# ACT copies a small sum out of the PSUM bank that the transposes share (convolution and two expert layers, one core)

## The chip, the cores and the metric

The kernel runs on one core of one Trainium2 chip. The metric is the device time of one execution in microseconds (us); the median of 3 runs stands for a kernel. The core has TensorE (PE, with its weight loads as PEld), VectorE (DVE), ScalarE (ACT), GpSimd (POOL) and the DMA queues, most of them issued by SyncE (SP). PE writes its results to PSUM, which has eight banks; this kernel gives each of them a fixed use.

## The reference, cut to what matters

```
attn: w = softmax(weight, over 7 taps), one filter per head (8 heads of 24 columns)
      x = causal 7-tap convolution of x[4, 3584, 192] with w          -> 14336 rows x 192
moe:  logits = x @ w_gate;  e = argmax;  gate = softmax(logits)[e]    (8 experts)
      out[row] = gate * (relu(x[row] @ w1[e]) @ w2[e])                w1 192x1024, w2 1024x192
moe2: the same with other weights, and a factor sigmoid(x @ w_output_gate)[e]
```

All arrays are float32. The weights w1 and w2 of both layers (16 experts' worth in all) have to be turned into pairs of 16-bit parts before the products can use them.

## The kernel before, in words

The kernel writes out by hand the order of the instructions on every engine. Each engine executes its own instructions in that order.

**Convolution, passes k = 0 to 36.** A pass multiplies four tiles of 112 rows with a band matrix on PE (`attend(k+1)`, L465). DVE finds each row's largest value and scales the rows (`split(k)`, L479 to L487, which empties the PSUM banks of `attend(k)`). ACT casts the scaled rows to 16 bits (`parts(k-1)`, L493), and POOL forms the low parts (L494, L495). Two passes later PE transposes the rows (`turn(k-3)`, L507), ACT empties the transposes' bank (`evacuate(k-3)`, L510), and PE makes logits (L517). The scaled rows `cxs` have two buffers; the cast rows `chl` have four.

**Slots.** After that the rows, sorted by expert, are worked off in 63 slots of up to 256 rows for each layer, so 126 slots. In slot u PE does `stage1(u)` (40 matmuls into four banks `ph`, L1134); ACT takes the positive part of each bank (L1136) and DVE the remainder (L1137). Then come the background work, `turn2(u-3)` (six transposes of the first layer's results into a bank `tp`, L1186), and `stage2(u-1)` (48 matmuls, L1150), in this order on PE. ACT empties `tp` (`evacuate2`, L1192) after the background work.

**Background work.** Two lists run beside the passes and slots. One routes rows to experts, mostly on DVE. The other prepares the weights of both layers, one unit (w1 or w2 of an expert) at a time: load; largest absolute values by ACT (L298); `scale`, which is `total` and `pow2`; scaling and splitting by ACT, POOL and DVE; store. The 16 units of layer 1 run during the convolution, where `scale` comes between `attend(k+1)` and `turn(k-3)` on PE, ahead of `split(k)` on DVE and ahead of `parts(k-1)` on ACT. The 16 units of layer 2 run during the first layer's slots, one in three slots, where `scale` comes after `stage1(u)` and the routing of that slot, and ahead of `turn2(u-3)`.

**The shared bank.** `total` sums the units' maxima over the 128 partitions with matmuls against ones (L145) into a tile of pool `rps` with tag `lg`. This pool has one buffer per tag. Under the tag `lg` stand `total`, the convolution's logits `lg`, the transposes `tp` of the slots, and the slots' logits `lg2`. Whoever writes next waits until the last reader has read. The first reader of `total` is the first line of `pow2` on DVE (L131, tile `wst`; for the gate weights L133, tile `gbt`).

```
self.rps = self.pool("rps", bufs=1, space=PSUM)
...
u.s, e = self.pow2(wp, self.total([u.am[:, c : c + 1] for c in range(NC)]), [P, 1], "ws")
...
bg(u, "A")
...
turn2(u - 3)
```

Of the kernel before, what the change touches and what calls it, by code (L numbers as in the profile page):

```python
# [11 lines left out]
F32 = mybir.dt.float32  # L12
# [5 lines left out]
P = 128  # L18
# [37 lines left out]
class Kern:  # L56
# [83 lines left out]
    def total(self, ams):  # L140

        n = ams[0].shape[-1]
        r = self.rps.tile([P, n], F32, tag="lg", name="total")
        for i, am in enumerate(ams):
            self.nc.tensor.matmul(r, lhsT=self.ones32, rhs=am, start=i == 0, stop=i == len(ams) - 1)  # L145
        return r

    def setup(self):
        nc = self.nc
# [1298 lines left out]
```

## Time and profile before

| what | value |
|---|---|
| median of 3 runs | 1360.57 us (1359.68 to 1361.41) |
| the profiled execution | 1359.16 us, span of its instructions 1357.2 us |
| PE busy | 1219.5 us, 90% of the span |
| DVE, ACT, POOL busy | 820.9 us, 637.8 us, 616.3 us |
| mean granted TensorE clock | 0.911 |
| convolution passes | from the first `attend` at 16.01 us to the last `evacuate` at 229.59 us |
| first `stage1` | 238.08 us |

The times in a trace count from the first instruction. A row of the timeline gives start and duration, engine, line, operation, the tile written and those read; in square brackets stands how long the engine had been idle before it, and what ended that. A tile's name is the program's with its buffer number left out.

### The profile page before, as it was taken

How to read it: one execution, taken by the hardware profiler on the slowest of the kernel's cores; microseconds unless marked ns; L12 is line 12 of the kernel's file. 1: busy time of each engine (PE TensorE's matmuls, PEld its weight loads, DVE VectorE, ACT ScalarE, POOL GpSimd, SP SyncE). 2: the span in 40 equal slices, each digit the busy share in tenths (PEclk: the TensorE clock that was granted, in tenths of full speed). 3: DMA queues.
4: the chain of work that ended last, by engine and by line, in shares of the span. 5: the costliest groups of instructions: out<-in, count | busy, mean ns of one | idle time of the engine just before them, and what ended most of it. 6: DMA issues, size and time to landing. Idle time of an engine off the chain costs nothing.

```text
span 1357.2 us, 36322 instructions
## 1 busy us (share of the span) xinstructions
PE 1219.5 (90%) x13032; PEld 1153.8 (85%) x13032; DVE 820.9 (60%) x2498; ACT 637.8 (47%) x1155; POOL 616.3 (45%) x673
## 2 busy tenths in 40 slices
PE   5788886979879998988997999999999998999997
PEld 4777776869879888878997999999999997899987
DVE  4777697877664745555457875588664444444442
ACT  2866663345446554665564444433333333333332
POOL 5534444325435544464454534444444446344442
PEclk9755556989889999989998999999999999999999
DMA  6997955555463779558684689765245465756375
GB/s 195 283 282 217 246 150 171 111 134 140 131 170 107 186 203 258 133 151 204 163 206 109 168 177 238 190 115 130 65 120 127 98 134 124 155 138 173 74 189 159
DMA packets 251087, 221.40 MB, mean 163 GB/s; under 512 B 144494, under 2 KB 220839, under 8 KB 250904
## 3 DMA queue, kind: packets, MB, share of 16 engines
q1 hardware_dynamic: 230556, 182.61, 51.3%
q0 software_dynamic: 17136, 34.68, 12.1%
q8 instruction: 106, 1.74, 0.6%
q10 hardware_dynamic: 3212, 1.74, 0.5%
q14 instruction: 77, 0.63, 0.2%
HBM read 275.60 MB, written 60.37 MB: 248 GB/s over the span
## 4 chain that ended last, share of the span: by engine, by line
PE 68%; DVE 19%; issue 4%; DMA 3%; ACT 2%; SPq 2%; POOL 1%; POOLq 0%; DVEq 0%; ACTq 0%
PE ph L1134 30%; PE py L1150 30%; PE cxp L465 4%; DVE h L1137 4%; DVE cxs L487 2%; PE tp L1186 1%; DVE cxp L479 1%; DMA wb<-wd 1%; DMA wb<-wdb 1%; DVE wh L334 1%; PE acc L968 1%; DVE eam L1160 1%; PE total L145 1%; ACT h L1136 1%; DMA mxt<-row 1%
## 5 line engine op out<-in xcount | busy, mean ns | idle before, releaser
L1134 PE MATMUL ph<-mxt,wb 128*128 128x256 f16 (+1 forms) x4840 | 535.2, 270 | 14.8 <-DMA wb<-wdb 6.5
L1134 PEld LDWEIGHTS <-wb 128*128 128x128 f16 x4840 | 455.9, 98 | 67.9 <-issue 9.0
L1150 PE MATMUL py<-wb,h 128*128 128x192 f16 x5592 | 492.5, 249 | 1.6 <-DMA wb<-wd 1.6
L1137 DVE SCALAR_TENSOR_TENSOR h<-ph,h 128x512 f16<-128x512 f32 x476 | 313.4, 686 | 277.2 <-ACT h L1136 273.5
L1150 PEld LDWEIGHTS <-h 128*128 128x128 f16 x5592 | 472.0, 99 | 5.2 <-issue 1.9
L1136 ACT ACTIVATE h<-ph 128x512 f16<-128x512 f32 x476 | 274.3, 595 | 148.4 <-PE ph L1134 143.5
L1050 POOL DMA_INDIRECT row<-rec,idx x238 | 232.1, 975 | 73.3 <-issue 41.0
L1233 POOL DMA_INDIRECT out_dram<-o,io x119 | 120.3, 1011 | 231.0 <-ACT o L1232 199.6
L1169 POOL TENSOR_TENSOR ehl<-exs,ehl 128x256 f16<-128x256 f32 (+1 forms) x63 | 42.6, 677 | 298.5 <-ACT ehl L1168 226.9
L1164 ACT ACTIVATE exs<-py,ess 128x192 f32<-128x192 f32 x119 | 43.9, 417 | 206.6 <-DVE ese L137 202.7
L1232 ACT ACTIVATE o<-py,sc 128x192 f32<-128x192 f32 x119 | 43.9, 417 | 205.6 <-PE py L1150 149.8
L465 PE MATMUL cxp<-x,tz 118*112 118x96 f32 x512 | 94.9, 371 | 38.5 <-DVE cxs L487 29.8
L465 PEld LDWEIGHTS cxp<-x,tz 118*112 118x112 f32 x512 | 88.2, 277 | 41.3 <-DVE cxs L487 31.8
L1160 DVE TENSOR_REDUCE eam<-py 128x2 f32<-128x384 f32 (+1 forms) x63 | 33.6, 533 | 134.9 <-PE py L1150 132.0
L338 POOL TENSOR_TENSOR wh<-wr,wh 128x768 f16<-128x768 f32 x48 | 79.8, 1663 | 50.2 <-ACT wh L326 26.0
L1186 PE MATMUL tp<-ident,ehl 128*128 128x128 f16 x357 | 31.7, 226 | 47.2 <-DVE wst L131 46.5
L510 ACT COPY cxt<-ctp 128x1344 f16<-128x1344 f16 x32 | 40.9, 1277 | 65.8 <-PE ctp L507 65.7
L1192 ACT COPY ext<-tp 128x768 f16<-128x768 f16 (+1 forms) x63 | 47.4, 752 | 46.6 <-PE tp L1186 46.6
L1186 PEld LDWEIGHTS <-ehl 128*128 128x128 f16 x357 | 27.1, 104 | 49.6 <-issue 47.0
L494 POOL TENSOR_TENSOR chl<-cxs,chl 112x512 f16<-112x512 f32 x32 | 40.4, 1261 | 54.1 <-ACT chl L493 43.2
L298 ACT ACTIVATE none<-wr 128x768 f16<-128x768 f32 x64 | 53.8, 840 | 1.0
L517 PEld LDWEIGHTS <-cxt 128*112 128x112 f16 x384 | 35.7, 192 | 5.0 <-issue 4.5
(203 smaller groups left out, 1077.9 us busy)
## 6 DMA issues: line engine op xcount, KB each, us to landing
wb<-wd SPq DMA_DIRECT2D x126, 768.0 KB
wb<-wda SPq DMA_DIRECT2D x126, 512.0 KB
wb<-wdb SPq DMA_DIRECT2D x126, 256.0 KB
wb<-wdb SPq DMA_DIRECT2D x126, 128.0 KB
wr<-in_moe_w_dram SPq DMA_DIRECT2D x16, 768.0 KB
wd<-wh SPq DMA_DIRECT2D x16, 768.0 KB
rec<-chl SPq DMA_DIRECT2D x32, 336.0 KB
rec<-ehl SPq DMA_DIRECT2D x56, 192.0 KB
```

The costliest lines, as they stand in the source:

```text
L298: nc.scalar.activation(none, u.r[:, c * CH : (c + 1) * CH], AF.Abs, scale=scale, accum_out=u.am[:, c : c + 1])
L338: nc.gpsimd.tensor_tensor(u.h[:, 1, q], u.r[:, q], u.h[:, 0, q], ALU.subtract)
L465: nc.tensor.matmul(to[:, :, hh * GD : (hh + 1) * GD], lhsT=self.tz[: self.KI, h, :], rhs=xin[b0][: self.KI, o : o + G, h * GD : (h + 1) * GD],
L1050: nc.gpsimd.indirect_dma_start(out=rw[:, :], out_offset=None, in_=rec[:, :], in_offset=bass.IndirectOffsetOnAxis(ap=idx, axis=0))
L1134: nc.tensor.matmul(ph[:, k, :], lhsT=l, rhs=xt[:, xb, 0:n], start=i == 0, stop=i == 4)
L1136: nc.scalar.activation(hi, ph, AF.Relu)
L1137: nc.vector.scalar_tensor_tensor(lo, in0=ph, scalar=0.0, in1=hi, op0=ALU.max, op1=ALU.subtract)
L1150: nc.tensor.matmul(py[:, c, 0:D], lhsT=h[:, f, a, c * P : (c + 1) * P], rhs=w[:, b, f, :], start=n == 0, stop=n == 3 * NCH - 1)
L1160: nc.vector.tensor_reduce(am, py, axis=AX.X, op=ALU.max, apply_absolute_value=True)
L1186: nc.tensor.transpose(tp[:, 3 * c + b], hl[:, c, b * P : (b + 1) * P], self.ident)
L1192: nc.scalar.copy(xt, self.sl[u].pop("tp"))
L1233: nc.gpsimd.indirect_dma_start(out=outs[q % NOUT][:, :], out_offset=bass.IndirectOffsetOnAxis(ap=io[:, 0:1], axis=0), in_=o, in_offset=Non ...
```

## The change

`total` gets a last step. ACT copies the sums from the PSUM tile to a small tile in SBUF (pool `ew`, four buffers), and `pow2` reads that tile. So the bank's reader is now ACT, and DVE reads the copy. `total` is called 34 times: once for each of the 32 units and once for each of the two sets of gate weights.

```diff
@@ def total(self, ams):
         r = self.rps.tile([P, n], F32, tag="lg", name="total")
         for i, am in enumerate(ams):
             self.nc.tensor.matmul(r, lhsT=self.ones32, rhs=am, start=i == 0, stop=i == len(ams) - 1)
-        return r
+
+        t = self.ew.tile([P, n], F32, tag=f"total{n}", name="sums")
+        self.nc.scalar.copy(t, r)
+        return t
```

## Rows read from the trace of the kernel before

**Rows 1.** Waits of PE, whole span: us in total, times, longest

```profile
PE tp L1186 <- DVE wst L131: 46.5, 16, 9.3
PE cxp L465 <- DVE cxs L487: 29.8, 21, 2.9
```

**Rows 2.** Timeline, the slot with the longest wait: start, us, engine, instruction

```profile
278.63 2.05 ACT L1136 ACTIVATE h<-ph 128x512 f16<-128x512 f32 x4
...
286.81 0.80 PE L1186 MATMUL tp<-ident,ehl 128*128 128x128 f16 x6 [9.33 <-DVE wst L131]
```

**Rows 3.** Timeline, a slot with a short wait

```profile
417.28 0.60 ACT L1136 ACTIVATE h<-ph 128x512 f16<-128x512 f32 x1 [0.49 <-PE ph L1134]
...
418.71 0.49 PE L1186 MATMUL tp<-ident,ehl 128*128 128x128 f16 x6 [1.13 <-DVE wst L131]
```

**Rows 4.** Timeline, six more slots with such a wait

```profile
350.61 0.80 PE L1186 MATMUL tp<-ident,ehl 128*128 128x128 f16 x6 [3.87 <-DVE wst L131]
...
388.07 0.80 PE L1186 MATMUL tp<-ident,ehl 128*128 128x128 f16 x6 [7.07 <-DVE wst L131]
...
472.85 2.05 ACT L1136 ACTIVATE h<-ph 128x512 f16<-128x512 f32 x4
...
476.07 0.49 PE L1186 MATMUL tp<-ident,ehl 128*128 128x128 f16 x6 [2.18 <-DVE wst L131]
...
535.88 0.49 PE L1186 MATMUL tp<-ident,ehl 128*128 128x128 f16 x6 [3.98 <-DVE wst L131]
...
613.94 0.49 PE L1186 MATMUL tp<-ident,ehl 128*128 128x128 f16 x6 [2.52 <-DVE wst L131]
...
726.88 2.05 ACT L1136 ACTIVATE h<-ph 128x512 f16<-128x512 f32 x4
...
734.18 0.80 PE L1186 MATMUL tp<-ident,ehl 128*128 128x128 f16 x6 [7.21 <-DVE wst L131]
```

**Rows 5.** Chain that ended last, by time: start, us, the second stage after such waits

```profile
287.61 5.51 PE py L1150 x48
...
351.41 6.02 PE py L1150 x48
...
388.87 6.06 PE py L1150 x48
...
476.57 3.96 PE py L1150 x48
...
536.37 5.62 PE py L1150 x48
...
614.43 5.61 PE py L1150 x48
...
734.97 5.40 PE py L1150 x48
```

**Rows 6.** Groups of ACT by shape: busy us, mean ns, idle before

```profile
L1164 ACT ACTIVATE exs<-py,ess 128x192 f32<-128x192 f32 x119 | 43.9, 417 | 206.6 <-DVE ese L137 202.7 <-DVE ess L136 3.9
...
L768 ACT ACTIVATE zs<-zs 128x16 f32<-128x16 f32 x7 | 1.4, 201 | 0.0
```

**Rows 7.** Timeline, two passes of the convolution

```profile
33.40 0.53 PE L145 MATMUL total<-wam,ones 128*128 128x1 f32 x4
...
34.85 0.84 ACT L298 ACTIVATE none<-wr 128x768 f16<-128x768 f32 x1
...
122.45 0.82 ACT L493 CAST chl<-cxs 112x768 f16<-112x768 f32 x1
...
126.73 0.98 PE L145 MATMUL total<-wam,ones 128*128 128x1 f32 x4 [3.02 <-DVE L L532]
...
127.75 0.16 DVE L131 TENSOR_SCALAR wst<-total 128x1 f32<-128x1 f32 x1 [0.24 <-PE total L145]
```

**Rows 8.** Waits of DVE, 0 to 232 us

```profile
DVE wst L131 <- PE total L145: 19.1, 13, 4.0
```

**Rows 9.** Busy time by engine after the longest wait: stretch, PE, PEld, DVE, ACT, POOL, clock, DMA

```profile
287.00:297.50 10.50, 10.50 (x101) 9.79 (x100) 4.38 (x14) 3.62 (x7) 1.71 (x3) 0.83 0.18 22
```

## The prediction, as it was put on record

> **What bounds the kernel now.** I first read the page: PE is busy nine tenths of the span, so what matters is where PE stands still. The view of PE's waits answers that. Its first row is the transposes of the slots, `tp`, waiting for DVE's `wst`: 46.5 us in 16 waits, the longest 9.3 us [rows 1]. Those are the 16 units of layer 2. Its second row belongs to the convolution: PE waits for DVE's `cxs` to empty a bank, 21 times [rows 1]. So in the slots PE sets the pace, and in the convolution PE and DVE wait for each other in turn.
>
> The timeline shows why the transposes wait. In a short case the last ACT instruction of the slot's first stage ends at 417.28 + 0.60 = 417.88; PE has been idle since 418.71 - 1.13 = 417.58, and goes on only when DVE, whose queue still holds its own work on that bank, has read the sums [rows 3]. In the longest case DVE has routing work in its queue too: PE is idle from 286.81 - 9.33 = 277.48 to 286.81, while ACT was through with the first stage at 278.63 + 2.05 = 280.68 [rows 2]. The data were ready at the start of each wait; the reader was late.
>
> PE pays a second time. After the longer waits the 48 matmuls of the second stage, which take 3.96 us after the wait of 2.18 us, take 5.40 to 6.06 us [rows 2, 4, 5]; in the stretch after the longest the granted clock was 0.83 of full, a mix of the levels 1.2 and 2.4 GHz [rows 9]. The six transposes take 0.80 us there in place of 0.49 [rows 2 to 4].
>
> **The change part by part.** *Removed:* DVE as the reader that frees the bank. *Added:* 34 ACT copies of one or two columns, and for each a wait of ACT for PE and a wait of DVE for ACT. No DMA and no matmul is added. The new tile has four buffers and one use per unit; units are slots or passes apart, so it makes nobody wait.
>
> *One copy.* The trace has no ACT copy of one column from PSUM. The nearest row below is an instruction on 16 columns, 0.20 us; the nearest above that reads PSUM is 0.42 us for 192 columns [rows 6]. One column lies near the first: 0.20 us, and 0.04 us for each signal between engines, as between the end of the sums at 126.73 + 0.98 = 127.71 and DVE's read of them at 127.75 [rows 7]. So PE can go on 0.28 us after both the sums and ACT's queue are ready (0.50 us at the upper end).
>
> *In the slots* the copy stands in ACT's queue behind the four instructions of the first stage. What is left of a wait is the time from PE's becoming idle to the end of the last of these, plus 0.28.
> - Short wait: 417.88 - 417.58 + 0.28 = 0.58 left of 1.13, so 0.55 saved [rows 3]. There are seven of 1.13 or 1.14: 3.85 us.
> - 9.33: 280.68 - 277.48 + 0.28 = 3.48 left, 5.85 saved [rows 2].
> - 7.21: idle from 726.97, ACT through at 728.93: 2.24 left, 4.97 saved [rows 4].
> - 2.18: idle from 473.89, ACT through at 474.90: 1.29 left, 0.89 saved [rows 4].
> - 3.87, 7.07, 3.98 and 2.52: by the pattern of the short wait 0.58 left of each, 3.29 + 6.49 + 3.40 + 1.94 = 15.12 saved [rows 4].
> - The other two wait 46.5 - 44.1 = 2.4 us together; by the same pattern 1.24 saved.
>
> The sum is 31.9 us; 14.6 us of waiting stay. With the copy at its upper end it is 3.5 us less.
>
> *Clock given back.* Where the wait shrinks to about 0.6 us, I take the second stage at 3.96 us: 2.06 + 2.10 + 1.66 + 1.65 for the waits of 3.87, 7.07, 3.98 and 2.52 [rows 5], and 0.31 for the transposes of the first two of them, 8.1 us. The 7.21 us wait shrinks to 2.24, nearest to the 2.18 that cost nothing: 1.44 + 0.31 more. The 9.33 us wait shrinks to 3.48, nearest to the 3.87 after which the clock was low: nothing. Together 9.8 us; the ends are 8.1 and, if the first comes free too, 11.7.
>
> *In the convolution* the same copy is a step more. DVE waits 13 times for the sums, 19.1 us in all [rows 8], so it is at `wst` before the sums are, and then `split(k)` is queued behind it, for which PE waits. Twelve of these passes get 0.24 us (copy and one signal): 2.9 us; the gate weights' call gets another 0.24. One pass is worse: the sums were ready at 33.40 + 0.53 = 33.93, and ACT's queue holds the instruction that ends at 34.85 + 0.84 = 35.69 ahead of the copy [rows 7]. DVE is held 1.9 us there; DVE waits for ACT soon after anyhow, so I count half, 1.0. The sum is 4.1 us. It is 0 if DVE's lateness is caught up, and about 8 with the copy at 0.42 and the full 1.9.
>
> In the same passes ACT now waits. Its queue has the copy ahead of `parts(k-1)`, whose cast ran at 122.45 while the sums ended at 127.71 [rows 7]: that cast moves back by 5.5 us. I cost this at nothing. What covers it: the cast rows are transposed two passes later, and the scaled rows have a second buffer; a pass takes (229.59 - 16.01) / 36, about 5.9 us. The transposes' bank is emptied after the cast, which then ends about when the transposes do. If that cover fails, see the second rival.
>
> One rule of the Trainium skill speaks against the change. "ScalarE: Activation LUTs", section "Rules for kernel authors", advises VectorE, not ScalarE, for plain arithmetic, for its speed per element. Followed here, the copy would stand in DVE's queue, the bank would come free no sooner than now, and the sum would stay at 1359 us. What the rows show to matter is whose queue is shorter, and that is ACT's in rows 2 and 3.
>
> **The sum.** The profiled execution took 1359.16 us, with 1.96 us outside its span, 1.41 us under the median. 1359.16 - 31.9 - 9.8 + 4.1 = 1321.6; beside the median that is 1323 us.
>
> **The rivals.**
>
> *DVE takes it back.* PE no longer waits at the transposes, but DVE's backlog, which made the long waits, is still there, and PE meets it one slot later, at the logits' gather or the next bank. If the five waits of 9.33, 3.87, 7.07, 3.98 and 7.21 gave nothing, 24.0 us of stall and 8.2 us of clock would be lost: 31.9 + 9.8 - 32.2 - 4.1 = 5.4 us gain, 1355 us; half of it back gives 1339. For it: DVE does work without a pause in the long waits. Against it: after the longest one DVE is busy 4.38 of 10.5 us [rows 9], so 6.1 us are free for the 5.85 that PE comes early, and the four `ph` banks let PE run ahead by a stage.
>
> *ACT's queue slows the convolution (slower).* The casts held behind the copy pass their delay on through POOL to `split`, which needs a buffer of scaled rows. If on average half the 5.5 us of the row above [rows 7] came through in each of 16 passes, that is 44 us: 1359.2 - 41.7 + 44 + 4.1 = 1365.6, beside the median 1367 us. It decides from about 2.4 us a pass. Against it stands the room of a pass in both buffers. The Trainium skill, "PSUM — Partial Sum Buffer", section "Engine vs sequencer instructions", calls the queues of ScalarE and VectorE strictly first in, first out; by it each such cast would wait for the sums, which is this rival's first step and the forecast's too.
>
> *The bank is not freed earlier.* If ACT reached its copy no sooner than DVE reaches `wst`, the slots would stay as they are and the convolution would pay: 1360.6 + 4.1, about 1365 us. Against it: in each slot of rows 2 to 4 for which both rows stand, ACT is through long before PE goes on.
>
> **How the numbers follow.** The forecast has 0.73, DVE taking back half or more 0.17, ACT's queue 0.05, no earlier release 0.05. The forecast's own range is 1315 (all the clock, no loss in the convolution) to 1334 (upper copy, lower clock, 8 us in the convolution). To leave out no more than 2 in 10 the range reaches halfway into the first rival's values and a little under the forecast's: 1314 to 1343. A measurement of this kernel tells 0.2%, 2.7 us, from no change. Faster takes the first two cases and nothing else: 0.90. The last two end slower, but with a part of the gain could end within 0.2%: same 0.04, slower 0.06.
>
> **What would show it.** In PE's waits the row of `tp` on `wst` is gone; in its place stands `tp` on ACT's copy with about 14.6 us. The second stage takes 3.96 us in all these slots but the first. DVE's `wst` waits for ACT's copy in the convolution, some 23 us in place of 19.1. The first `stage1` starts about 4 us later than 238.08. The casts L493 have idle time before them that PE's sums ended, without more waiting of DVE or PE for POOL. The prediction is wrong if the first `stage1` is late by far more, if PE has new waits for `ph` banks, for `L` (DVE's gather) or for weights' DMAs in the slots after 281, 347 or 382 us, or if the low clock stays after short waits.

## The result, and the profile after

The changed kernel takes 1323.02 us (median of 4 runs, 1322.37 to 1323.69) against 1360.99 us beside it; the ratio is 0.9712, 95% interval 0.9681 to 0.9743. Its profiled execution has a span of 1320.7 us, 36.5 us less than before, and a mean granted clock of 0.920.

The waits of PE over the whole span of the changed kernel (us in total, times, longest) answer to [rows 1]:

```profile
PE cxp L468 <- DVE cxs L490: 33.9, 23, 3.4
PE tp L1189 <- ACT sums L148: 11.0, 16, 2.5
...
PE lg L1203 <- ACT ext L1195: 6.3, 4, 2.6
```

The last row, the slots' logits waiting for ACT to empty the transposes, was 4.5 us in 3 waits before:

```profile
PE lg L1200 <- ACT ext L1192: 4.5, 3, 2.6
```

The transposes now wait for ACT's copy, 11.0 us in place of 46.5. The timeline of a short case shows how, beside [rows 3]:

```profile
400.38 0.60 ACT L1139 ACTIVATE h<-ph 128x512 f16<-128x512 f32 x1 [0.49 <-PE ph L1137]
400.87 0.15 ACT L148 COPY sums<-total 128x1 f32<-128x1 f32 x1
...
401.08 0.49 PE L1189 MATMUL tp<-ident,ehl 128*128 128x128 f16 x6 [0.39 <-ACT sums L148]
...
401.62 0.14 DVE L131 TENSOR_SCALAR wst<-sums 128x1 f32<-128x1 f32 x1
```

ACT's copy starts 0.11 us before the instruction ahead of it ends, takes 0.15 us, and 0.06 us after it PE goes on: 0.39 us of waiting. DVE reads the copy 0.54 us after PE has gone on; before the change PE waited for that read. The longest case, beside [rows 2]:

```profile
282.71 2.05 ACT L1139 ACTIVATE h<-ph 128x512 f16<-128x512 f32 x4
...
284.64 0.18 ACT L148 COPY sums<-total 128x1 f32<-128x1 f32 x1
284.87 0.49 PE L1189 MATMUL tp<-ident,ehl 128*128 128x128 f16 x6 [2.52 <-ACT sums L148]
```

Here ACT itself is late, and 2.52 us stay. The chain of the changed kernel has two second stages above 5 us, beside [rows 5]:

```profile
255.02 5.64 PE py L1153 x48
...
699.02 5.61 PE py L1153 x48
```

Five of the six slow ones of [rows 5] are gone; the one after the last unit's wait, 2.08 us now, is still slow, and the one at 255.02 is new. These rows of the timeline show what was new between:

```profile
379.96 0.73 ACT L1167 ACTIVATE exs<-py,ess 128x192 f32<-128x192 f32 x2 [7.17 <-DVE ese L137]
...
386.85 0.30 PE L1203 MATMUL lg<-gbwt,ext 128*128 128x32 f16 x6 [1.81 <-ACT ext L1195]
...
552.83 5.78 PE L1153 MATMUL py<-wb,h 128*128 128x192 f16 x48
```

The first two belong together: one slot after the 7.07 us wait that went, ACT has stood idle 7.17 us behind DVE's backlog, so it has not yet emptied the transposes when PE comes to the logits, and PE waits 1.81 us. The third is a second stage at a low clock (at full clock this view gives 4.12), without a wait for the sums ahead of it.

Where the 36.5 us went, by the starts of rows in both timelines: the first `stage1` starts at 241.13 in place of 238.08 (+3.05); from there to the first transposes it is 32.05 in place of 30.23 (+1.82, nearly all of it the slow stage at 255.02); from the first transposes to those of the last unit it is 425.35 in place of 465.87 (-40.52); the rest is 622.17 in place of 623.02 (-0.85).

In the convolution, DVE's and ACT's waits of the changed kernel up to 236 us, beside [rows 8]:

```profile
DVE wst L131 <- ACT sums L148: 26.3, 14, 4.2
DVE wh L337 <- ACT wh L331: 8.3, 6, 1.7
```

```profile
ACT sums L148 <- PE total L145: 44.7, 16, 5.2
ACT cxt L513 <- PE ctp L510: 23.8, 27, 4.5
```

The second and fourth of these were, in the kernel before:

```profile
DVE wh L334 <- ACT wh L328: 10.7, 7, 3.0
```

```profile
ACT cxt L510 <- PE ctp L507: 65.7, 25, 5.6
```

DVE waits 26.3 us for the sums in place of 19.1, but its wait for ACT's scaled weights (`wh`) has gone from 10.7 to 8.3 us. ACT waits 44.7 us for PE's sums, with the casts behind it; but it waits 41.9 us less for PE's transposes, which it empties afterwards. POOL, which works on the casts, waits 80.1 us for them in place of 43.2, and there the lateness ends: DVE waits for POOL once, 2.9 us, as before. The pass that the prediction singled out [rows 7], after:

```profile
33.23 0.53 PE L145 MATMUL total<-wam,ones 128*128 128x1 f32 x4
...
34.51 0.84 ACT L301 ACTIVATE none<-wr 128x768 f16<-128x768 f32 x1
...
35.35 0.14 ACT L148 COPY sums<-total 128x1 f32<-128x1 f32 x1
...
35.53 0.15 DVE L131 TENSOR_SCALAR wst<-sums 128x1 f32<-128x1 f32 x1 [3.69 <-ACT sums L148]
```

The sums end at 33.76 and DVE reads them at 35.53, 1.8 us later, as was counted. From the scaled rows of this early stretch, pass 0, to those of pass 8 it is 4.4 us longer than before. Busy time by engine in it, before and after (stretch, PE, PEld, DVE, ACT, POOL, clock, DMA):

```profile
20.70:53.90 33.20, 26.81 (x281) 25.76 (x280) 23.83 (x55) 25.54 (x37) 17.26 (x19) 0.85 0.97 279
```

```profile
20.60:58.20 37.60, 31.07 (x281) 30.01 (x279) 23.79 (x55) 25.99 (x40) 16.60 (x19) 0.72 0.96 270
```

PE is busy 4.3 us longer with the same 281 matmuls, at a granted clock of 0.72 in place of 0.85, and stands still as long as before.

### The profile page after: what moved, and what is told of

Its sections match the earlier page's. It is cut to its first block, busy times and chain, and to the rows that moved or that the text cites. A ratio compares the mean times of both kernels' runs of the same rounds, so it can differ in the third digit from the quotient of the medians.

```text
span 1320.7 us, 36349 instructions
## 1 busy us (share of the span) xinstructions
PE 1214.5 (92%) x13032; PEld 1148.7 (87%) x13032; DVE 819.2 (62%) x2498; ACT 641.2 (49%) x1189; POOL 614.5 (47%) x673
## 4 chain that ended last, share of the span: by engine, by line
PE 68%; DVE 16%; DMA 5%; ACT 4%; issue 4%; POOL 2%; SPq 1%; POOLq 0%; DVEq 0%; ACTq 0%
PE ph L1137 31%; PE py L1153 29%; PE cxp L468 4%; DVE h L1140 2%; DMA wb<-wdb 2%; DVE cxs L490 2%; DVE cxp L482 1%; PE tp L1189 1%; ACT h L1139 1%; DMA row<-rec,idx 1%; DVE wh L337 1%; PE acc L971 1%; PE total L145 1%; DMA mxt<-row 1%; DVE eam L1163 1%
## 5 line engine op out<-in xcount | busy, mean ns | idle before, releaser
L1153 PE MATMUL py<-wb,h 128*128 128x192 f16 x5592 | 487.2, 248 | 0.4 <-DMA wb<-wd 0.4
L1153 PEld LDWEIGHTS <-h 128*128 128x128 f16 x5592 | 467.3, 99 | 3.0 <-issue 0.5
L497 POOL TENSOR_TENSOR chl<-cxs,chl 112x512 f16<-112x512 f32 x32 | 37.4, 1168 | 88.5 <-ACT chl L496 80.1
L520 PE MATMUL lg<-gawt,cxt 128*112 128x16 f16 x384 | 35.6, 227 | 5.3 <-DVE L L535 3.6
```

Source lines behind the costliest of these rows:

```text
L520: nc.tensor.matmul(lg[:CT, g, :], lhsT=xt[:, g * 3 + b, :], rhs=self.ga[0][:, 1 if b == 1 else 0].rearrange("p a e -> p (a e)"), start=b == 0,
L1153: nc.tensor.matmul(py[:, c, 0:D], lhsT=h[:, f, a, c * P : (c + 1) * P], rhs=w[:, b, f, :], start=n == 0, stop=n == 3 * NCH - 1)
```

## The experiments

The theory: PE waits because the transposes need the bank that holds the sums, and what counts is how soon the bank's reader comes up in its own queue; the copy costs the convolution a little. The rivals: the gain has to do with what `pow2` reads, or with the convolution; DVE's backlog is only met elsewhere; the convolution's loss comes from the casts; waits count by their length alone.

The kernel before took 1392 to 1397 us in the experiments' sessions, so a kernel's time is given as its ratio to the kernel before in the same session, with the 95% interval in brackets. An expectation in us is meant for a kernel before of 1360.57 us.

**The copy in the slots alone, and in the convolution alone.**

```diff
+        if not self.attended:      # slots only; the other kernel has: if self.attended
+            return r
         t = self.ew.tile([P, n], F32, tag=f"total{n}", name="sums")
         self.nc.scalar.copy(t, r)
         return t
```

> The copy by ACT is made only in the slots (units of layer 2); during the convolution DVE reads the sums from the bank, as before the change. Forecast's theory (ACT frees the shared bank sooner in the slots, and the copy costs the convolution a step): the first stage1 starts at 238 us as before the change (241 after it), the transposes' wait stays near 11 us, and the time is 3 to 5 us under the changed kernel, 1318 to 1320 us. Rival (the copy in the convolution costs nothing, the later first slot has another cause): 1323 us and a first stage1 at 241.

Measured: 0.9708 (0.9660 to 0.9757), first `stage1` at 236.33 us. Both expected times, 1318 to 1320 us (0.969 to 0.970) and 1323 us (0.972), lie in the interval.

> The other half: the copy by ACT only during the convolution and for the gate weights; in the slots DVE reads from the bank. Forecast's theory: nothing is gained, the transposes wait 46 us as before, and the convolution loses 3 to 5 us: 1364 to 1366 us. Rival (part of the gain comes from the convolution): under 1358 us.

Measured: 0.9999 (0.9975 to 1.0024), first `stage1` at 241.10 us. Its waits of PE:

```profile
PE tp L1191 <- DVE wst L131: 47.3, 16, 8.6
```

The whole gain is made in the slots. What the copy costs the convolution is at most 0.24% by the ratio, which is 3.3 us; that it costs nothing is as well within the interval, while the 3 to 5 us that were expected (1.0025 to 1.004) lie above it. The kernel with the copy in the slots alone was run again, beside the changed one:

> The changed kernel itself, beside the next three on one chip. Ratio to the kernel before 0.971 as first measured; first stage1 at 241 us.

Measured: 0.9721 (0.9691 to 0.9751), first `stage1` at 243.51.

> The copy only in the slots, once more beside the changed kernel. Forecast's theory (the copy costs the convolution some 3 us): ratio 0.002 to 0.004 under the changed kernel's, first stage1 2 to 4 us sooner. Rival (the convolution's loss is made up elsewhere or is chance): the same ratio within 0.001.

Measured: 0.9700 (0.9675 to 0.9725). That is 0.0021 under the changed kernel, as the forecast's theory expected, or 2.6 us (1355.59 against 1358.17), but the intervals overlap; and its first `stage1` came at 244.84, later than that of the changed kernel, where it was expected 2 to 4 us sooner. So the question stays open here; see the table below.

**DVE makes the copy.**

```diff
-        self.nc.scalar.copy(t, r)
+        self.nc.vector.tensor_copy(t, r)
```

> The same small tile, but DVE makes the copy. Forecast's theory (what counts is in whose queue the bank's reader stands): the transposes wait for DVE's copy about 46 us, and 34 more DVE instructions of about 0.15 us go on top: 1360 to 1365 us. Rival (it is enough that pow2 no longer reads PSUM, whoever copies): 1320 to 1330 us.

Measured: 1.0017 (1.0002 to 1.0031). Its waits of PE:

```profile
PE tp L1189 <- DVE sums L148: 46.5, 15, 8.5
```

The wait is the old one under a new name, and 0.17% is 2.3 us. So it is the queue that counts, not the copy: the rival falls. The rule of the Trainium skill that the prediction weighed ("ScalarE: Activation LUTs", section "Rules for kernel authors": plain arithmetic on VectorE), taken over to this copy, leads here to the slower kernel, 1.0017 against 0.9712.

**Another bank in place of a copy.** In the slots the sums go into a tile of the second stage's pool, whose two banks are used in turn, and DVE reads them there as late as it likes.

```diff
-        r = self.rps.tile([P, n], F32, tag="lg", name="total")
+        if self.attended:
+            r = self.pyp.tile([P, NSUB, T], F32, tag="py", name="total")[:, 0, 0:n]
+        else:
+            r = self.rps.tile([P, n], F32, tag="lg", name="total")
...
-        t = self.ew.tile([P, n], F32, tag=f"total{n}", name="sums")
-        self.nc.scalar.copy(t, r)
-        return t
+        return r
```

> No copy at all. In the slots the sums go into a tile of the second stage's pool (py, two banks) in place of the transposes' bank, and DVE reads them there as late as before; in the convolution all is as before the change. Theory of the shared bank (PE waits only because the transposes need the bank that holds the sums): the wait of the transposes for the sums is gone, the convolution is as before, 1307 to 1313 us. Rival (PE really needs DVE to have come that far, and would wait for DVE's backlog elsewhere, at py or ph): 1340 us or more, with new waits of py or ph for DVE.

Measured: 0.9666 (0.9627 to 0.9705). Of PE's waits the first row is that of the convolution, and there is no wait of the transposes for the sums; the two other rows have grown:

```profile
PE cxp L469 <- DVE cxs L491: 29.5, 21, 3.4
...
PE lg L1204 <- ACT ext L1196: 9.3, 6, 2.6
...
PE tp L1190 <- DVE L L1215: 3.4, 4, 1.2
```

The ratio is 1315 us beside 1360.57, a little above the 1307 to 1313 that the theory expected and far below the rival's 1340.

> The sums in a bank of py in the slots and no copy, once more beside the changed kernel. Theory of the shared bank: ratio 0.004 to 0.010 under the changed kernel's, since the 11 us that the transposes still wait there are gone and so is the convolution's step. Rival (the gain first seen against another chip's figures was the chip's): the same ratio within 0.002.

Measured: 0.9660 (0.9631 to 0.9689), median 1349.84 us, 8.3 us under the changed kernel's in that session. DVE's backlog is as large as before, and PE runs past it: in the first of the two profiles DVE reads the 16 units' sums 43.9 us after they end, added up, and in the kernel before 43.3. The rival that DVE takes the gain back is left with the row `lg`, where PE waits 9.3 us in place of the 4.5 us of the kernel before, and with DVE's reading of the logits, `L`, at the transposes, 3.4 us in place of 0.7.

**Longer waits in the slots.** Four, or two, copies of a scratch tile by ACT ahead of the sums' copy, in the slots only (the tile is set up once at the start).

```diff
+        if self.attended:
+            for _ in range(4):     # the other kernel: 2
+                late = self.ew.tile([P, 768], F16, tag="late", name="late", bufs=1)
+                self.nc.scalar.copy(late, self.late)
         self.nc.scalar.copy(t, r)
```

> The changed kernel with four ACT copies of 128x768 (scratch, about 0.7 us each back to back) ahead of the sums' copy, in the slots only, so that every transposes' wait grows by about 2.8 us, to 3.2 us in the short cases. Theory with the clock (a wait of this length also costs some 2 us of TensorE at its lower level afterwards): 45 us of stall and 20 to 35 us of clock over the changed kernel, ratio to the kernel before 1.02 to 1.03, and most of the 16 second stages after the waits take 5.4 to 6.1 us. Rival (only the wait itself counts): 45 us, ratio 1.005, second stages at 3.96.

Measured: 1.0252 (1.0212 to 1.0292). PE's wait, and two of the 16 second stages behind the waits in the timeline, the longest and the shortest:

```profile
PE tp L1195 <- ACT sums L152: 65.1, 16, 5.9
```

```profile
392.43 6.42 PE L1159 MATMUL py<-wb,h 128*128 128x192 f16 x48
...
624.35 4.86 PE L1159 MATMUL py<-wb,h 128*128 128x192 f16 x48
```

All 16 are slower than 4.12 us, by 28 us together. Over the changed kernel's 0.9712 the ratio rose by 0.054, 73 us, give or take 7; the waits grew by 65.1 - 11.0 = 54.1, more than the 45 that were expected. So some 20 us are not wait, and the clock is where they are: 0.90 of full from 240 to 780 us, against 0.98 in the changed kernel from 240 to 700.

> The same with two such copies: waits grow by 1.4 us, to 1.8 us in the short cases, under the 2.18 us that cost no clock in the kernel before. Theory with the clock: 22 us of stall over the changed kernel, ratio 0.987 to 0.990, second stages at 3.96 us except after the two longest waits. Rival (every wait costs clock in proportion): ratio 0.995 or more.

Measured: 0.9981 (0.9957 to 1.0006). The expectation of the theory with the clock, that waits of 1.8 us cost no clock, is wrong, and the ratio is one that the rival expected. PE's wait, and rows of the chain behind waits of exactly 1.99 us:

```profile
PE tp L1195 <- ACT sums L152: 34.7, 15, 4.1
```

```profile
379.74 5.25 PE py L1159 x48
410.43 5.27 PE py L1159 x48
440.86 5.42 PE py L1159 x48
...
502.69 5.21 PE py L1159 x48
...
644.36 5.62 PE py L1159 x48
...
704.17 5.19 PE py L1159 x48
```

Ten waits of 1.99 us have the second stage right behind the transposes; six of these stages take 5.19 to 5.62 us, the other four 3.96. So it is not the rival's proportion either. The ratio rose by 0.027, 37 us, of which the waits are 34.7 - 11.0 = 23.7. A wait of 2 us may cost clock or not, and its length alone does not tell.

The changed kernel's two profiles show this without any edit between them. The last unit's slot, first in the profile of the result, then in the second one:

```profile
698.53 0.49 PE L1189 MATMUL tp<-ident,ehl 128*128 128x128 f16 x6 [2.08 <-ACT sums L148]
698.86 5.78 PE L1153 MATMUL py<-wb,h 128*128 128x192 f16 x48
```

```profile
700.33 0.49 PE L1189 MATMUL tp<-ident,ehl 128*128 128x128 f16 x6 [2.08 <-ACT sums L148]
700.66 4.12 PE L1153 MATMUL py<-wb,h 128*128 128x192 f16 x48
```

The same instructions wait the same 2.08 us; then the granted clock is 0.70 over the second stage in one execution and 1.00 in the other.

**The convolution: later sums, earlier casts.** In the first kernel ACT holds the copy back by about 1.7 us, in the convolution only. In the second, which is otherwise the changed kernel, the cast of the pass before is issued ahead of the background work.

```diff
+        if not self.attended:
+            self.nc.scalar.copy(self.ew.tile([P, n], F32, tag=f"first{n}", name="first"), r)
+            for _ in range(2):
+                late = self.ew.tile([P, 768], F16, tag="late", name="late", bufs=1)
+                self.nc.scalar.copy(late, self.late)
         self.nc.scalar.copy(t, r)
```

> The changed kernel with 1.6 us more between the sums and their copy in the convolution only (a first copy of the sums to scratch, two copies of 128x768, then the copy). Forecast's theory (DVE's read stands on the path of the convolution, each pass pays for the step): 17 times 1.6, up to 27 us, over the changed kernel, first stage1 at 260 to 268 us, ratio 0.985 to 0.991. Rival (DVE and ACT take the lateness back within the pass): under 8 us, ratio 0.971 to 0.977.

Measured: 0.9877 (0.9833 to 0.9921), first `stage1` at 262.82. One pass in its timeline:

```profile
164.96 0.16 ACT L149 COPY first<-total 128x1 f32<-128x1 f32 x1 [3.08 <-PE total L145]
165.02 1.70 ACT L152 COPY late<-lates 128x768 f16<-128x768 f16 x2
166.62 0.15 ACT L153 COPY sums<-total 128x1 f32<-128x1 f32 x1
166.81 0.15 DVE L131 TENSOR_SCALAR wst<-sums 128x1 f32<-128x1 f32 x1 [2.99 <-ACT sums L153]
```

Ratio and first `stage1` are those of the forecast's theory: some 1.7 us more at each of 17 calls (29 us) cost about 20 us. The late copy also frees the bank late, and the convolution's logits wait for it 15.0 us (1.1 us in the changed kernel); so it is shown that a late copy is paid for, and not which of the two waits pays. In this pass PE, done with the logits, stands still another 1.82 us until DVE has scaled the rows, which speaks for DVE's read.

```diff
+            if 1 <= k < NG + 1:
+                parts(k - 1)
             bg("B")
...
                 split(k)
-            if 1 <= k < NG + 1:
-                parts(k - 1)
...
```

> The changed kernel, with the cast of the pass before (parts) issued ahead of the background work, so that ACT does it before it waits for the sums. Forecast's theory (the late casts are covered by the second buffers): the same time as the changed kernel within 2 us, first stage1 at 241 +-1.5. Rival (the late casts are what costs the convolution its 3 us): first stage1 at 238 or sooner and 3 us less in all.

Measured: 0.9680 (0.9657 to 0.9703), median 1352.66 us, 5.5 us under the changed kernel's in that session; first `stage1` at 238.78. The forecast's theory had expected no more than 2 us; by this run alone the rival would stand.

**Both.** To see whether the earlier cast only undoes the wait for the sums, it was put into the kernel that has no copy:

```diff
# the kernel with the sums in a bank of py, and
+            if 1 <= k < NG + 1:
+                parts(k - 1)
             bg("B")
...
                 split(k)
-            if 1 <= k < NG + 1:
-                parts(k - 1)
```

> No copy, the sums in a bank of py in the slots, and the cast of the pass before issued ahead of the background work in the convolution. If the earlier cast helps by itself (its own place in ACT's and POOL's queues): the passes 8 to 31 take 161 us as in the run with both the copy and the earlier cast, in place of 165, and the ratio is 0.962 to 0.964. If it only undid the cast's wait for the sums: 165 us and 0.966 as without it.

Measured: 0.9609 (0.9578 to 0.9641), 1337.85 us where the kernel before takes 1391.96. It is the fastest of all. With no copy in the convolution, the earlier cast still helps, and by more than was expected: so it helps by its own place in the queues, and that it helps says nothing for the rival that the late casts cost the changed kernel its time.

The convolution in all these profiles, from the timelines (start of the first `stage1`; from `cxs` of pass 8 to that of pass 31):

| kernel | copy in the convolution | first stage1, us | passes 8 to 31, us |
|---|---|---|---|
| before | no | 238.1 | 165.3 |
| slots alone, twice | no | 236.3, 244.8 | 163.6, 164.9 |
| bank of py, twice | no | 239.2, 240.1 | 165.9, 164.5 |
| changed, twice | yes | 241.1, 243.5 | 164.2, 165.6 |
| convolution alone | yes | 241.1 | 165.2 |
| four, two late copies in the slots | yes | 242.5, 240.9 | 165.2, 164.1 |
| copy by DVE | by DVE | 240.9 | 166.5 |
| late copies in the convolution | late | 262.8 | 184.1 |
| changed, cast first | yes | 238.8 | 160.9 |
| bank of py, cast first | no | 233.3 | 158.1 |

From pass 8 on the copy costs nothing that shows: the mean is 164.8 us over the five profiles without it and 164.9 over the five with it. The first `stage1` is at 239.7 us in the mean without, at 241.8 with it; the five without differ by 8.5 us among themselves, most of it before pass 8. There the time goes with the clock: from pass 0 to pass 8 the five without take 33.2 to 40.3 us at a granted clock of 0.85 down to 0.67, the five with it 35.8 to 38.4 us at 0.81 down to 0.72. The last two rows of the table are the one place where a cost of the copy may be seen behind pass 8: with the cast issued first, 160.9 us with the copy and 158.1 without. That is one profile each, at granted clocks of 0.55 and 0.63, and the five without the copy scatter by 2.3 us; so it does not show the cost either.

## Why the prediction was right

**The mechanism.** PE waited for the reader of a shared bank, not for data. Shown from both sides: with a reader that comes sooner the wait falls, with the copy in DVE's queue it stays at 46.5 us, and with the sums in another bank the wait goes though DVE reads as late as ever.

**Stalls: 31.9 us were forecast, 35.5 were saved.** The short cases keep 0.39 us, not 0.58: the copy takes 0.15 us, not 0.20, and overlaps the end of the instruction before it. The Trainium skill, "ScalarE: Activation LUTs", section "What ACT_TABLE_LOAD costs", has such an overlap of about 93 ns for ACTIVATE instructions back to back; here the second is a copy, and the row at 400.87 shows 0.11 us. The longest wait kept 2.52 us, not 3.48.

**Clock: 9.8 us were forecast.** Leaving out the last unit's slot, the second stages behind the waits became 9.0 us shorter, and the transposes 0.9 us; in the last slot nearly nothing changed. The size was right, the step behind it was not: I took each remaining wait's cost from the row with the nearest length. The wait that became 2.52 us, costed at the low clock, came free; the one that became 2.08, counted as free, cost 1.65 us, and in the second profile of the same kernel nothing; of ten waits of 1.99 us in the experiment six cost some. The sign that was named, 3.96 us in all these slots but the first, came out the other way: the first is fast and the last slow. Two errors of opposite sign met in the sum: that is luck. Slow second stages also appeared at 255.02 and 552.83, 1.7 us too long each, where no term stood.

**DVE takes it back: 0 was forecast, with a chance of 0.17 for half or more.** One slot later PE waits 1.81 us at the logits, because ACT stands behind DVE; that and the slow stages after 552 us are most of the difference between the 45.4 us that waits, second stages and transposes gave back and the 40.5 us that are gained between the first and the last unit.

**The convolution: +4.1 us were forecast.** The profile shows +3.05 us at the first `stage1`, but the profiles without the copy scatter by more than that, and it did not come about as the sum has it: up to pass 8 the profile is 4.4 us longer, as much as PE is busy longer at the lower clock, and from there to pass 31 it is 1.1 us shorter. Two profiles without the copy have a clock as low, so it is not shown that the copy brought it.

Of the parts of the sum, the single pass with its 1.8 us is there: from its scaled rows to the next it is 7.8 us in all five profiles with the copy, where four of the five without take 5.9 to 6.6. So most of the lateness came through, where half was counted. The first gate weights' call was costed at 0.24 us and came 3.7 us later (ACT comes to its copy at 12.19, and DVE reads at 12.38 in place of 8.68); nothing was lost by it, for the first scaled rows start at 20.6 as against 20.7 before. The 0.24 us in each of the other passes may be in DVE's wait for the sums, which grew by 7.2 us, but are not in the time from pass 8 on. A lateness of 1.7 us a call does come through, with some 0.5 us a call taken back, so there is room for the copy's 0.2 and not for much more; DVE's shorter wait for ACT's scaled weights (8.3 in place of 10.7 us) is where I would look for it, which is argued and not shown. The cost of the copy in the convolution is between nothing and 3.3 us by the ratio; it stays open where in that.

**The casts held back** by ACT's wait for the sums, 44.7 us in all, cost nothing that shows, as was forecast: passes 8 to 31 are as long with the copy as without. The room was larger than counted: a pass takes 165.3 / 23 = 7.2 us there, not 5.9, and ACT's wait for the transposes, the step behind the cast, fell by 41.9 us, so most of what ACT now waits for the sums it no longer waits there. ACT's queue behaves as the section "Engine vs sequencer instructions" of the Trainium skill's "PSUM — Partial Sum Buffer" has it, strictly in order: while ACT waited those 44.7 us, no cast behind a copy started ahead of it.

So the total is as good as exact partly by luck: 3.6 us more stall saved and 1 us less lost ahead of the slots than forecast, and in exchange about 6 us of small new losses that had no term. The two ends of the forecast's own range are not quite what its terms give, either: beside the median they come to 1317 and 1332 us, not 1315 and 1334.

## What to carry to other kernels

Where an engine waits for a bank or buffer, ask who reads it last and what stands ahead of that reader in its own queue; a tiny copy by an engine with a shorter queue frees it. A tile in a bank that is free at that time does so without the copy, and was better here by 8 us. Price a wait of the tensor engine with the clock behind it, as a chance rather than a threshold. A wait that an added instruction brings to an engine holds everything queued behind it: check that those have a buffer to spare, and try them ahead of it.

## What the runs showed of the hardware that was not expected

Equal waits of TensorE (1.99 us, in slots of the same make) were followed by 48 matmuls at 3.96 us four times and at 5.19 to 5.62 us six times; and one and the same wait of 2.08 us of one kernel was followed by a granted clock of 0.70 in one execution and of 1.00 in another. What decides it stays open. In the kernel with four late copies, the waits of 3.52 us and more were followed by a slow stage each of 16 times (4.86 to 6.42 us, where full clock gives 4.12 in that view). An ACT copy of one column from PSUM takes 0.14 to 0.18 us in these rows, and in the rows above starts about 0.1 us before the instruction ahead of it ends.
